# Four buffers for blocks of x, one for loaded q/k, and softmax divisors turned by DMA, in a fused top-k attention and quick-GELU feed-forward kernel

## The chip, the cores and the metric

The kernel runs on one core of one Trainium2 chip. The metric is the device time of one execution in microseconds (us), as the median of several runs. A profiled execution gives a page of tables and a trace. Engines are named as in the profile: PE (TensorE matmul), PEld (its weight load), DVE (VectorE), ACT (ScalarE), POOL (GpSimd), SP (SyncE, which here only issues DMAs, strictly one after the other).

## The reference

Attention over 8 batches, 8 heads, 576 positions and 64 channels that keeps the 32 largest scores of each row, then a feed-forward layer on the joined heads:

```python
scores = (q @ k.T) / sqrt(64)
kth = np.partition(scores, -32, axis=-1)[..., -32:-31]
scores = np.where(scores >= kth, scores, -1e9)
attn = exp(scores - max);  attn = attn / (sum(attn) + 1e-9)
x = (attn @ v)                      # (8, 8, 576, 64) -> (4608, 512)
h = x @ w_in                        # 512 -> 2048
g = h * (1 / (1 + exp(-1.702 * h)))
out = g @ w_out                     # 2048 -> 512
```

Everything is float32.

## The kernel before

**Slots.** The attention is cut into 144 slots, 18 for each batch `b`. A full slot is 128 query rows of two heads (a head pair, `hp` 0 to 3). The last 64 rows of a head pair share a slot with those of another pair. Four full slots with the same 128 rows give one block of x, transposed: a tile `xT` of 128 x 4 x 128 (channels by rows). The 64-row ends of two batches give a block `xT_t`. A block is 128 tokens for the feed-forward layer, and there are 36 of them.

**What a slot does.** PE multiplies q by k into PSUM (`scores`, L281), ACT copies the scores out (`copy_scores`, L293), and DVE finds the 32 largest of each row with MAX8 and MATCH_REPLACE8 on pairwise greater and lesser halves (`topk_of_pairs`, L336, L339; `pair_up`, L322 on DVE and L325, L326 on POOL). ACT then masks (L387) and exponentiates (L390), which also leaves the sums of each row in `sums`. `split` (L461) separates the 16-bit halves, and a DMA writes them to DRAM (`rows`, L463). `turn_by_dma` (L469) reads them back with a DMA transpose into `pt`, which has two buffers. PE multiplies `pt` by v into `o` (`values_at`, L526). These are not yet divided by the sums.

**The divisors.** `invert` (L420, L422 on DVE) makes the reciprocals of the sums of two slots, 128 x 4 numbers with the query row on the partition. The values in `o` lie transposed, with the query row along the free dimension and the channel on the partition, so the divisors have to be turned and repeated over 64 partitions. Before the change POOL repeats them over 64 columns (`wide`, L424), and PE turns that with a transpose per slot (`sum_rows`, L515) into the same PSUM tile as `o`. ACT copies both out to `x` (L902, 128 x 512), and POOL multiplies one by the other into `xT` (`x_of`, L544).

**The feed-forward layer.** `hidden` (L575) multiplies a quarter of `w_in` (16 matmuls of 128 x 128) by the first block in the list `ready`, into PSUM `ph`. ACT takes the tanh (L592) and copies `ph` to `h` (L595), POOL makes the gate from them (`gate`, L604, L605; DVE in the last slots, L607), and PE multiplies it by `w_out` (`project`, L622). A block leaves `ready` after its fourth `hidden`, and its buffer is free then.

**Order.** Each engine's order is written out by hand; nothing is reordered. After an opening and 12 single slots (`slot`), `two_slots(n)` handles slots n and n+1, 68 times from n=12 on. I call one such round a period. On PE a period runs: `hidden`, `project`, the two transposes L515, scores of n+2, values of n-3 and n-2, scores of n+3, `hidden` (into another PSUM pool), `project`. On SP it runs: loads of the first slot, `rows` of n-1, the four DMAs of `prepare_by_dma` if one is due, the transpose `pt` of n-1, the transpose of a prepared q/k pair, loads of the second slot, `rows` of n, `pt` of n, and outputs between them. On POOL the multiplication `x_of` stands between a gate and the next `lesser` (L325, L326). In it `x_of` of a block that begins takes a new `xT` buffer, and with two buffers it waits until PE has done the last `hidden` of the block before the last. At the end `last_slot` works off the remaining blocks.

**Loads of q and k.** `load_both` brings q and k of a head pair (six DMAs) into a tile of the pool `loads`, two buffers. `prepare_by_dma` splits their halves on ACT (L239), writes them to DRAM (L243 to L248) and reads them back transposed (L252). `FETCH` and `READY` (`FETCH_1`, `READY_1` for batch 1) give the slots, counted back from a batch's first slot, in which each pair is loaded and prepared. The pool `raws`, eight buffers, holds `lesser`, `h`, `wide` and `x` in turn.

Of the kernel before, what the change touches and what calls it, by code (L numbers as in the profile page):

```python
# [11 lines left out]
F32 = mybir.dt.float32  # L12
# [4 lines left out]
DRAM = bass.MemoryType.DRAM  # L17

P = 128
# [11 lines left out]
def kernel(  # L31
# [27 lines left out]
    nc = tc.nc  # L59

    B, H, S, D = q.shape
# [3 lines left out]
    NF = S // P  # L65
# [23 lines left out]
    const = ctx.enter_context(tc.tile_pool(name="const", bufs=1))  # L89
    pool = lambda name, bufs, **kw: ctx.enter_context(tc.tile_pool(name=name, bufs=bufs, **kw))  # L90
    raws = pool("raws", 8)
    loads = pool("loads", 2)
    vals = pool("vals", 6)
    qkt = pool("qkt", 6)
    scp = pool("scp", 4)
# [1 line left out]
    lefts = pool("lefts", 2)  # L97
    small = pool("small", 4)
    ptp = pool("ptp", 2)
    xtp = pool("xtp", 2)  # L100
    xtt = pool("xtt", 1)
    thp = pool("thp", 5)
    apart = pool("apart", 4, space=DRAM)
    apart_qk = pool("apart_qk", 2, space=DRAM)
    ps_s = pool("ps_s", 2, space=PSUM)
    ps_t = pool("ps_t", 2, space=PSUM)
    ps_h = pool("ps_h", 1, space=PSUM)
# [2 lines left out]
    ident = const.tile([P, P], F32, name="ident")  # L110
# [6 lines left out]
    raw = {}  # L117
# [42 lines left out]
    loaded = {}  # L160
# [10 lines left out]
    def load(name, b, hp, queue=None):  # L171

        src = q if name == "q" else k
        if (b, hp) not in loaded:
            loaded[b, hp] = loads.tile([P, 2 * NF + 1, 2, D], F32, name="qk_l")
        t = loaded[b, hp]
        if queue is None:
            heads_of = lambda j: of_load(name, t)[:, :, j, :]
        else:
            heads_of = lambda j: heads_apart(name, t)[:, j, :, :]  # L180
        queue = queue or nc.sync
        for j in range(2):
            queue.dma_start(heads_of(j), src[b, 2 * hp + j, 0:FULL, :].rearrange("(p t) d -> p t d", t=NF))

        on = slice(0, TAIL) if name == "q" else slice(TAIL, P)
        queue.dma_start(t[on, 2 * NF, :, :], src[b, 2 * hp : 2 * hp + 2, FULL:S, :].rearrange("h p d -> p h d"))
# [218 lines left out]
    sums = {}  # L405
# [8 lines left out]
    def invert(n):  # L414

        k = (n + 1) // 2
        if k in sums:
            count = 2 if 2 * k < N else 1
            total = sums[k][:, 0:count, :]
            nc.vector.tensor_scalar_add(total, total, 1e-9)  # L420
            inverse = small.tile([P, 2 * count], F32, name="inverse")
            nc.vector.reciprocal(inverse[:], total.rearrange("p s j -> p (s j)"))  # L422
            wide = sums[k] = raws.tile([P, 2, 2, D], F32, name="wide", tag="raw")
            nc.gpsimd.tensor_copy(  # L424
                out=wide[:, 0:count, :, :].rearrange("p s j d -> p (s j) d"),
                in_=inverse[:].unsqueeze(2).to_broadcast([P, 2 * count, D]),
            )

    def turn(n, first, blocks):
        pr = st[n]["pr"]  # L430
# [78 lines left out]
        else:  # L509
            put_off.append(bring)  # L510


    def sum_rows(m, to):

        nc.tensor.transpose(to, sums[(m + 1) // 2][:, (m + 1) % 2, :, :], ident[:])  # L515

    def values_at(m, o):

        b, t, hps = slots[m]
        pt = st[m]["pt"]  # L520
        for p in range(2 if t == NF else 1):
            cols = slice(p * TAIL, (p + 1) * TAIL) if t == NF else slice(0, P)
            main, tail = vv[b, hps[p]]
            for c in range(NF + 1):
                for j in range(2):
                    nc.tensor.matmul(  # L526
                        o[j * D : (j + 1) * D, cols],
                        lhsT=main[:, j, c, :] if c < NF else tail[:, j, :],
                        rhs=pt[:, MAIN[j] + c if c < NF else NF, cols],
                        start=(c == 0),  # L530
                        stop=(c == NF),
                    )
        st[m].clear()
# [32 lines left out]
    def hidden(into=None):  # L566
        if not ready:
            return
        xT, rows = ready[0]
        g = hidden_at["g"]  # L570
        ph = (into or ps_h).tile([P, G, P], F32, name="ph", tag="tp" if into else "ph")
        for i in range(G):
            f = g * G + i
            for c in range(CC):
                nc.tensor.matmul(  # L575
                    ph[:, i, :],
                    lhsT=win[:, c, f * P : (f + 1) * P],
                    rhs=xT[:, c, :],
                    start=(c == 0),
                    stop=(c == CC - 1),  # L580
                )
        to_gate.append((ph, g, rows))
        hidden_at["g"] = (g + 1) % NG
        if g == NG - 1:
            ready.pop(0)

    def tanh(aside):

        if to_gate:
            ph, g, rows = to_gate.pop(0)  # L590
            th = thp.tile([P, G, P], F32, name="th")
            nc.scalar.activation(th[:], ph[:], AF.Tanh, scale=0.851 / RAISE)  # L592
            if aside:
                h = raws.tile([P, G, P], F32, name="h", tag="raw")
                nc.scalar.copy(out=h[:], in_=ph[:])  # L595
                ph = h
            gated.append((th, ph, g, rows))

    def gate(aside):
        if not gated:  # L600
            return
        th, h, g, rows = gated.pop(0)
        if aside:
            nc.gpsimd.tensor_scalar(th[:], th[:], 1.0, 1.0, op0=ALU.add, op1=ALU.mult)  # L604
            nc.gpsimd.tensor_tensor(out=th[:], in0=th[:], in1=h[:], op=ALU.mult)  # L605
        else:
            nc.vector.scalar_tensor_tensor(  # L607
                out=th[:], in0=th[:], scalar=1.0, in1=h[:], op0=ALU.add, op1=ALU.mult
            )
        to_project.append((th, g, rows))  # L610
# [39 lines left out]

    READY = (-12, -10, -4, -2)
    READY_1 = (-6, -4, -3, -2)
    FETCH = (-16, -14, -8, -6)
    FETCH_1 = (-12, -10, -5, -3)
    VALUES = (-2, -1, 1, 2)
    by_slot = dict(enumerate([2, 2, 3, 3, 3, 3, 3, 3, 3, 3, 2, 2]))
    for n in by_slot:
# [170 lines left out]
    def last_slot():  # L828

        tanh(False)  # L830
        gate(False)
        if may_project(0):
            project(range(G))
        hidden()

    def two_slots(n):

        first, second = [later.pop(m, []) for m in (n, n + 1)]
        live = lambda m: 0 <= m < N
        aside = n < N  # L840

        def begin(todo):
            for fn, args in todo:
                if fn is not prepare_by_dma:
                    fn(*args)

        def prepare_some(todo):
            for fn, args in todo:
                if fn is prepare_by_dma:
                    fn(*args)  # L850

        def find(m):
            for i, op in enumerate(topk_of_pairs(m) if live(m) else [lambda: None] * 23):
                op()
                if i == 8 and m % 2 == 0:
                    invert(m - 2)
                if i > 1 and unfinished:
                    finish_one()

        def project_one():  # L860
            if may_project(0):
                project(range(G), True)

        def measure(m):
            if live(m):
                bounds(m)
            gate(aside)

        begin(first)
        measure(n - 1)  # L870
        if live(n - 1):
            exponentials(n - 1)
            split(n - 1)
        bring_all()
        find(n)
        hidden()
        project_one()
        tanh(aside)
        prepare_some(first)
        held = [m for m in (n - 3, n - 2) if live(m) and "rows" in st[m]]  # L880
        o = ps_t.tile([P, 2, 2, P], F32, name="o", tag="tp") if held else None
        for i, m in enumerate(held):
            sum_rows(m, o[:, i, 0, :])
        if live(n + 2):
            scores(n + 2)
            copy_scores(n + 2)
        leave_all()
        for i, m in enumerate(held):
            values_at(m, o[:, i, 1, :])
        if live(n - 1):  # L890
            turn_by_dma(n - 1)
        while turns:
            turns.pop(0)()
        if live(n + 3):
            scores(n + 3)
        begin(second)
        measure(n)
        if live(n):
            exponentials(n)
        if held:  # L900
            x = raws.tile([P, 2, 2, P], F32, name="x", tag="raw")
            nc.scalar.copy(out=x[:, 0 : len(held)], in_=o[:, 0 : len(held)])  # L902
            for i, m in enumerate(held):
                x_of(m, x[:, i, 1, :], x[:, i, 0, :])
        if live(n):
            split(n)
            turn_by_dma(n)
        hidden(ps_t)
        if live(n + 3):
            copy_scores(n + 3)  # L910
        tanh(aside)
        prepare_some(second)
        project_one()
        leave_all()
        find(n + 1)
# [40 lines left out]
```

## Time and profile before

| | us |
|---|---|
| median of 3 runs | 1561.03 (1560.61 to 1563.05) |
| profiled execution | 1561.79 |
| its span, first to last instruction | 1560.0 |
| PE busy | 1461.0 (94%) |
| DVE busy | 1375.2 (88%) |
| ACT busy | 1171.5 (75%) |
| POOL busy | 888.9 (57%) |
| mean granted TensorE clock | 0.972 |

The span is some 1.8 us shorter than the time of the same execution. Busy shares are means over stages. The opening and the 12 single slots take about the first 150 us, the periods run until about 1500 us, and the last slots take the rest. The start of the pair of transposes L515 marks a period on PE, and the distance from one to the next is its length. An idle time in square brackets in a timeline stands in front of the instruction, with what ended it.

### The profile page before, as it was taken

The numbers are of one execution on the slowest core, as the hardware profiler recorded it, in microseconds if no ns is written. First come the engines' busy times: TensorE is split into PE (matmuls) and PEld (weight loads), VectorE is DVE, ScalarE is ACT, GpSimd is POOL, SyncE is SP. The second block draws the span as 40 slices with busy tenths as digits, with TensorE's granted clock in tenths as the row PEclk, the third lists the DMA queues.
The fourth block names the chain that finished last, engine by engine and source line by source line (L and its number), as shares of the span: only waits on it lengthen the run. The fifth ranks groups of instructions, "written<-read, shape, count | busy, mean of one in ns | idle before, by whom it ended". The sixth has DMA issues, their size and how long they took to land. (4 is left out here: it accounts for less than half of the span.)

```text
span 1560.0 us, 31382 instructions
## 1 busy us (share of the span) xinstructions
PE 1461.0 (94%) x10729; PEld 1059.6 (68%) x10729; DVE 1375.2 (88%) x4542; ACT 1171.5 (75%) x1846; POOL 888.9 (57%) x1119
## 2 busy tenths in 40 slices
PE   7789789999999899999998899999998899999997
PEld 5667556777766577777776577777775677777765
DVE  7999989999989799999997799999997889999700
ACT  6998778888768687878786687888876688777710
POOL 3788555666645566666665466666664566666400
PEclk8899899999999999999999999999999999999999
DMA  7451786767755486677767576676765658444500
GB/s 241 134 160 36 194 214 184 194 172 183 189 156 162 126 199 173 173 176 181 187 162 161 128 186 190 163 189 175 179 172 146 161 147 203 131 128 130 145 23 14
DMA packets 533778, 248.35 MB, mean 159 GB/s; under 512 B 465136, under 2 KB 507889, under 8 KB 533617
## 3 DMA queue, kind: packets, MB, share of 16 engines
q1 hardware_dynamic: 533184, 246.05, 60.3%
q8 instruction: 84, 1.38, 0.4%
q14 instruction: 78, 0.63, 0.1%
q10 hardware_dynamic: 432, 0.30, 0.1%
HBM read 45.09 MB, written 105.32 MB: 96 GB/s over the span
## 5 line engine op out<-in xcount | busy, mean ns | idle before, releaser
L622 PE MATMUL po<-wout,th 128*128 128x512 f32 x1152 | 534.2, 608 | 43.9 <-POOL th L605 35.4
L575 PEld LDWEIGHTS ph<-xT,win 128*128 128x128 f32 x4096 | 473.9, 192 | 69.6 <-issue 53.2
L575 PE MATMUL ph<-xT,win 128*128 128x128 f32 x4096 | 489.3, 277 | 12.3 <-POOL xT L544 12.3
L622 PEld LDWEIGHTS po<-wout,th 128*128 128x128 f32 x1152 | 213.5, 195 | 264.5 <-issue 216.4
L336 DVE MAX8 top<-left 128x8 f32<-128x288 f32 x792 | 325.3, 445 | 0.0
L461 ACT COPY sc<-pr 128x2304 uint16<-128x2304 uint16 x133 | 281.5, 2117 | 2.2
L293 ACT ACTIVATE sc<-s_ps 128x576 f32<-128x576 f32 x288 | 172.2, 654 | 140.6 <-PE s_ps L281 130.3
L544 POOL TENSOR_TENSOR xT<-x 128x128 f32<-128x128 f32 x117 | 51.7, 458 | 392.6 <-DVE top L343 215.1
L390 ACT ACTIVATE pr<-sc,low 128x576 f32<-128x576 f32 x288 | 220.6, 774 | 47.7 <-POOL low L367 47.7
L336 DVE MAX8 top<-lesser 128x8 f32<-128x288 f32 x528 | 214.1, 446 | 37.1 <-POOL lesser L326 37.1
L339 DVE MATCH_REPLACE8 left<-top,left 128x288 f32<-128x288 f32 x528 | 229.6, 442 | 0.0
L387 ACT ACTIVATE sc<-sc,cut 128x576 f32<-128x576 f32 x288 | 208.7, 783 | 2.7 <-POOL cut L378 2.1
L326 POOL TENSOR_TENSOR lesser<-lesser,greater 128x576 int32<-128x576 int32 x132 | 186.0, 1409 | 22.7 <-DVE greater L322 13.2
L325 POOL TENSOR_TENSOR lesser<-sc 128x576 int32<-128x576 int32 x132 | 187.6, 1421 | 0.0
L281 PE MATMUL s_ps<-qk_t 64*128 64x288 f32 (+1 forms) x1280 | 185.2, 436 | 1.0 <-ACT sc L293 0.8
L605 POOL TENSOR_TENSOR th<-th,h 128x512 f32<-128x512 f32 x127 | 161.9, 1275 | 10.6
L526 PE MATMUL o<-pt,v_l 128*64 128x128 f32 (+1 forms) x2384 | 147.5, 268 | 11.0 <-DMA pt<-rows 11.0
L526 PEld LDWEIGHTS o<-pt,v_l 128*64 128x64 f32 x2384 | 122.7, 139 | 38.1 <-issue 22.9
L592 ACT ACTIVATE th<-ph 128x512 f32<-128x512 f32 x144 | 86.6, 602 | 81.0 <-PE ph L575 80.9
L322 DVE TENSOR_TENSOR greater<-sc 128x576 f32<-128x576 f32 x132 | 104.6, 792 | 44.7 <-ACT sc L293 35.4
L281 PEld LDWEIGHTS s_ps<-qk_t 64*128 64x128 f32 (+1 forms) x1280 | 100.8, 180 | 42.6 <-issue 22.1
L339 DVE MATCH_REPLACE8 left<-top,greater 128x288 f32<-128x288 f32 x264 | 114.8, 442 | 0.0
(86 smaller groups left out, 1606.2 us busy)
## 6 DMA issues: line engine op xcount, KB each, us to landing
rows<-sc SPq DMA_DIRECT2D x133, 576.0 KB, 3.1
qk_rows<-halves SPq DMA_DIRECT2D x56, 256.0 KB, 2.8
qk_l<-in_q_dram SPq DMA_DIRECT2D x64, 128.0 KB, 3.0
raw<-in_moe_w_in_dram SPq DMA_DIRECT2D x16, 512.0 KB, 5.2
v_l<-in_v_dram SPq DMA_DIRECT2D x32, 256.0 KB, 3.2
raw<-in_moe_w_out_dram SPq DMA_DIRECT2D x16, 512.0 KB, 3.6
out_dram<-ob SPq DMA_DIRECT2D x32, 256.0 KB, 2.9
qk_l<-in_k_dram SPq DMA_DIRECT2D x62, 128.0 KB, 2.9
```

The lines of the kernel that those rows point to most:

```text
L281: nc.tensor.matmul(ps[i][rows, c, 0:HALF], lhsT=qT[b, hps[p]][on, cols], rhs=kT[b, hps[p]][on, FIRST[i] + c * HALF : FIRST[i] + (c + 1) * ...
L293: nc.scalar.mul(out=to, in_=ps[i][:, :, 0:HALF], mul=SCALE)
L325: nc.gpsimd.tensor_tensor(out=whole, in0=a.bitcast(I32), in1=b.bitcast(I32), op=ALU.add)
L326: nc.gpsimd.tensor_tensor(out=whole, in0=whole, in1=greater[n][:].bitcast(I32), op=ALU.subtract)
L336: nc.vector.max(top[:, i, 8 * r : 8 * r + 8], src[:, i, :])
L339: nc.vector.match_replace(to[:, i, :], top[:, i, 8 * r : 8 * r + 8], src[:, i, :], LOWEST)
L387: nc.scalar.activation(sc[:, i, :], sc[:, i, :], AF.Prelu, bias=cut[:, i : i + 1], alpha=HUGE)
L390: nc.scalar.activation(pr[:, i * S : (i + 1) * S], sc[:, i, :], AF.Exp, bias=low[:, i : i + 1], accum_out=den[:, i : i + 1],)
L461: nc.scalar.copy(out=halves, in_=pr[:].bitcast(U16).rearrange("p (k h) -> p h k", h=2))
L526: nc.tensor.matmul(o[j * D : (j + 1) * D, cols], lhsT=main[:, j, c, :] if c < NF else tail[:, j, :], rhs=pt[:, MAIN[j] + c if c < NF else ...
L575: nc.tensor.matmul(ph[:, i, :], lhsT=win[:, c, f * P : (f + 1) * P], rhs=xT[:, c, :], start=(c == 0), stop=(c == CC - 1),)
L622: nc.tensor.matmul(po[:], lhsT=gT[:, i, :], rhs=wout[:, f, :], start=(f == 0), stop=(f == FC - 1))
```

## The change

`xtp`, the pool of `xT`, gets four buffers in place of two, and `loads` one in place of two. In batch 0 the loads of odd head pairs go into the pool of `pt`, whose buffers have the same size. `FETCH` and `FETCH_1` move so that each load follows the preparation of the pair before it.

The divisors are no longer repeated by POOL and transposed by PE. `invert` issues a DMA on SP that writes the 128 x 4 reciprocals to DRAM (`lines`) with the query row along the line. The new function `spread` issues two DMAs on SP that read these lines back, each repeated over 64 partitions, into a tile `by` of the pool `raws`. The PSUM tile `o` and its copy `x` halve to 128 x 256.

In `last_slot` the next `hidden` comes ahead of the gate and `project` of the one before, and the two take turns in two PSUM pools.

```diff
-    loads = pool("loads", 2)
+    loads = pool("loads", 1)
-    xtp = pool("xtp", 2)
+    xtp = pool("xtp", 4)
+    apart_by = pool("apart_by", 2, space=DRAM)
...
-            loaded[b, hp] = loads.tile([P, 2 * NF + 1, 2, D], F32, name="qk_l")
+            home, tag = (ptp, "pt") if b == 0 and hp % 2 else (loads, "qk_l")
+            loaded[b, hp] = home.tile([P, 2 * NF + 1, 2, D], F32, name="qk_l", tag=tag)
...
-            wide = sums[k] = raws.tile([P, 2, 2, D], F32, name="wide", tag="raw")
-            nc.gpsimd.tensor_copy(
-                out=wide[:, 0:count, :, :].rearrange("p s j d -> p (s j) d"),
-                in_=inverse[:].unsqueeze(2).to_broadcast([P, 2 * count, D]),
+            lines = apart_by.tile([2, 2, P], F32, name="lines")
+            nc.sync.dma_start(lines[0:count].rearrange("s j q -> q (s j)"), inverse[:])
+            sums[k] = lines, count
+
+    def spread(n):
+
+        lines, count = sums.pop((n + 1) // 2)
+        by = raws.tile([P, 2, P], F32, name="by", tag="raw")
+        for j in range(2):
+            nc.sync.dma_start(
+                by[j * D : (j + 1) * D, 0:count, :],
+                lines[0:count, j, :].unsqueeze(0).to_broadcast([D, count, P]),
             )
+        return by
...
-    def sum_rows(m, to):
-
-        nc.tensor.transpose(to, sums[(m + 1) // 2][:, (m + 1) % 2, :, :], ident[:])
...
-    FETCH = (-16, -14, -8, -6)
-    FETCH_1 = (-12, -10, -5, -3)
+    FETCH = (-16, -11, -8, -3)
+    FETCH_1 = (-12, -5, -3, -2)
...
     def last_slot():
 
         tanh(False)
+        hidden(ps_t if hidden_at["g"] % 2 else None)
         gate(False)
         if may_project(0):
             project(range(G))
-        hidden()
...
-        o = ps_t.tile([P, 2, 2, P], F32, name="o", tag="tp") if held else None
-        for i, m in enumerate(held):
-            sum_rows(m, o[:, i, 0, :])
+        by = spread(held[0]) if held else None
+        o = ps_t.tile([P, 2, P], F32, name="o", tag="tp") if held else None
...
-            values_at(m, o[:, i, 1, :])
+            values_at(m, o[:, i, :])
...
-            x = raws.tile([P, 2, 2, P], F32, name="x", tag="raw")
+            x = raws.tile([P, 2, P], F32, name="x", tag="raw")
...
-                x_of(m, x[:, i, 1, :], x[:, i, 0, :])
+                x_of(m, x[:, i, :], by[:, (m + 1) % 2, :])
```

## The prediction

> **What bounds the kernel now.** I read the page first: PE is busy for 94% of the span. Then the waits, for what stops PE, and the timeline, for where. The lines below come in that order: page, waits, three windows (length, then busy time of PE, PEld, DVE, ACT, POOL, granted clock, DMA share, GB/s), and pieces of the timeline.
>
> ```profile
> PE 1461.0 (94%) x10729; PEld 1059.6 (68%) x10729; DVE 1375.2 (88%) x4542; ACT 1171.5 (75%) x1846; POOL 888.9 (57%) x1119
> ...
> qk_l<-in_q_dram SPq DMA_DIRECT2D x64, 128.0 KB, 3.0
> ```
>
> ```profile
> POOL xT L544 <- PE ph L575: 55.4, 6, 9.2
> PE po L622 <- POOL th L605: 35.4, 7, 5.8
> ```
>
> ```profile
> 448.30:475.40 27.10, 21.28 (x140) 14.80 (x139) 20.40 (x72) 18.29 (x25) 12.61 (x16) 0.87 0.56 150
> 1120.95:1140.05 19.10, 19.10 (x140) 13.92 (x139) 18.77 (x67) 15.09 (x24) 10.82 (x14) 1.00 0.78 192
> 1407.60:1427.70 20.10, 19.30 (x155) 13.65 (x154) 19.67 (x69) 15.21 (x24) 10.79 (x14) 1.00 0.41 109
> ```
>
> ```profile
> 829.04 0.45 POOL L544 TENSOR_TENSOR xT<-x 128x128 f32<-128x128 f32 x1 [9.21 <-PE ph L575]
> ...
> 834.78 5.78 PE L622 MATMUL po<-wout,th 128*128 128x512 f32 x8 [5.83 <-POOL th L605]
> ```
>
> ```profile
> 1061.34 0.35 SPq L463 DMA_DIRECT2D rows<-sc  x1
> 1062.54 0.38 PE L515 MATMUL o<-ident,wide 128*128 128x128 f32 x2
> 1062.85 1.24 PE L281 MATMUL s_ps<-qk_t 64*128 64x288 f32 x8
> 1065.38 2.83 SPq L469 DMA_TRANSPOSE pt<-rows  x1
> 1068.05 0.57 ACT L902 COPY x<-o 128x512 f32<-128x512 f32 x1
> 1068.70 0.88 POOL L544 TENSOR_TENSOR xT<-x 128x128 f32<-128x128 f32 x2 [4.82 <-DVE top L343]
> 1077.22 1.41 POOL L326 TENSOR_TENSOR lesser<-lesser,greater 128x576 int32<-128x576 int32 x1
> 1077.85 0.82 DVE L343 TENSOR_TENSOR top<-top 128x32 f32<-128x32 f32 x1
> ```
>
> ```profile
> 186.10 1.26 SPq L183 DMA_DIRECT2D qk_l<-in_q_dram  x2
> 187.75 2.13 ACT L239 COPY halves<-qk_l 128x2304 uint16<-128x2304 uint16 x1
> 1517.69 3.70 PE L622 MATMUL po<-wout,th 128*128 128x512 f32 x8 [1.41 <-DVE th L607]
> ```
>
> The starts of the L515 pairs give 66 period lengths, of three kinds. Most take 19.11, and PE has no gap in them (second window): PE is the bound, and DVE, at 18.77, is right behind. Sixteen take about 20.1: `hidden` follows in the same period on the block that `x_of` has just finished, and PE waits some 0.7 for it. Six take 27.07, 27.83, 27.27, 27.93, 27.32 and 27.95: there POOL waits for an `xT` buffer (9.21 above), everything behind it on POOL is late, and PE ends 5.8 idle and goes on at a lower clock (0.87 in the first window). The first few periods, to about 254, are not full on PE and go by SP, ACT and DVE.
>
> **The change part by part.**
>
> **1. Four `xT` buffers.** In the order written out, the six long periods are those in which a block begins one period before the block two places earlier has had its last `hidden`. With four buffers the block that must be gone is two older, gone four or more periods before. The wait then has no cause. The six lengths sum to 165.37, against 6 x 19.11 = 114.66: **-50.7**. Where does the stall go? Into PE, whose periods on both sides already last 19.11 without a gap. This takes the loss of clock with it.
>
> **2. No L515, no `wide`.** From the first L515 to the scores behind it is 1062.54 to 1062.85, 0.31. It is on PE's path in the 62 periods or so after 254: at most 19.2. DVE could cap this at 18.77. But its merge L343 takes 0.82 there beside POOL's L326, and 0.19 at 1068.52, where POOL rests, so it can lose 0.63; `wide` takes up to 0.96 on POOL just ahead and L326 moves up by as much as that goes. If the divisors are late by part of a microsecond the merge stays long, and only 19.11 - 18.95 = 0.16 is had, 18.95 being two DVE searches of 9.21 and 9.98 (starts 800.33, 810.31, 819.52) less their 0.24 of waits. Between 9.9 and 19.2 I take **-15**, nearer the upper end because in most periods `by` is in time by item 4. The smaller `x` copy is on ACT, which has over 3 us idle in a period: nothing.
>
> **3. The last slots.** Five times PE waits 1.41 for tanh and gate (1517.69 and every 8.68 after). With the next `hidden` in front, 3.6 of matmuls cover this; behind the last one lies the `project` before it, 3.4. Without that cover it would be 1.41 each again. **-7.05**.
>
> **4. Divisors through DRAM.** Per period SP gains three DMAs: `lines` behind `rows` of n-1, `by` twice behind the q/k DMAs, and the `by` issue waits until `lines` has landed. Queued behind it on SP are an output, `pt` of n-1 and the q/k transpose. `pt` of n-1 moves from 1065.38 to about 1066.3 and is wanted by PE one period later: covered by some 12 us. `pt` of n, which is nearest to its use, has about 2.6 us left in the periods with loads of item 5.
> The one that waits for `by` is POOL's `x_of`, at 1068.70. No row shows `lines` (512 runs of 4 bytes). The nearest is a q load, also 512 runs: 3.0 from issue to landing, 0.62 to issue. Below I bound it by the shortest landing of the page, 2.1, above by the q/k transpose, 5.0. `by` has 64 KB in 512-byte runs, nearest the small loads at 2.6 to 2.7. From `rows` at 1061.34: `lines` issued at 1061.75; behind `rows` on the same queue, so I add 0.4 to 3.1, the landing of `rows`: 3.5; second `by` issued 0.5 later; 2.7 to land: 1068.45. The margin is 0.25. Ends: 2.1 and 2.1 give 1066.4, 2.3 early; 5.0 and 5.0 give 1072.2, 3.5 late. Lateness L counts fully in the sixteen just-in-time periods; in the others POOL has cover until DVE wants `lesser`: L326 ends at 1072.44 and is read at 1075.43, so some 2.9. In the six of the sixteen with a q/k preparation ahead of `by` (qk_rows issued 1081.52 to 1083.74), `by` is issued at 1083.8 to 1084.8 and lands at about 1087.5, against `x_of` at 1087.80. I take 0.3 for each of sixteen: **+5**, ends 0 and, with 3.5, 56 plus 50 x 0.6 = 30, so 86.
>
> The Trainium skill, "DMA: Bandwidth & Descriptors", speaks against this: "Rules for kernel authors" says that a strided last dimension becomes one descriptor per element, and "Bandwidth" gives about 10.5 ns per packet, beside some 2.0 us fixed. My estimate from the page is 512 x 10.5 ns = 5.4, so 7.4 for `lines`, and `by` would be late by 3.65: 16 x 3.65 + 50 x 0.75, some 96 us, in place of 5. The trace argues otherwise: 465136 packets under 512 bytes go almost wholly to 161 transposes, over 2700 each, landed in 4.8 to 5.0. Whether 4-byte writes behave so, no row here shows.
>
> **5. One buffer for loads.** In batches 2 to 7 a load sits in the period before its preparation. Loads at -11 and -3 move to the second half and go ahead of `rows` of n: six DMAs of 0.6 delay that by some 3 us, `pt` of n to a landing near 1101.7 where PE wants it near 1104.3. Covered: 0, and 12 x 2 = 24 if the cover is gone. In batch 1 pairs 2 and 3 are loaded in the very slot of their preparation. Before, ACT's L239 ran at 187.75; now the load can only be issued at about 187.6 and lands near 194: 6 us in which ACT stands, with the score copies behind it and DVE waiting for those. The next pair adds some 3. DVE is near its limit there, so this counts, less what SP catches up meanwhile (PE also waits 6.0 for a `pt` at 225). Ends 0 and 14: **+7**. In batch 0 one short SP wait goes: nothing.
>
> Sum: 1560.0 - 50.7 - 15 - 7.05 + 5 + 7 = 1499.2. The profiled execution took 1.8 more than its span and the median 0.8 less than that: **1500**.
>
> **The rivals.**
>
> *Divisors late.* `lines` and `by` both at 5.0: 1500 + 86 - 5 = 1581 at the very end; at 3.8 for both, lateness is 1.4: 16 x 1.4 = 22 in place of 5, 1517. I put it at **1540**, lateness 2.7. For it: 0.25 of margin. Against: small DMAs here land in 2.1 to 3.1.
>
> *Loads late.* Item 5 at its upper ends, 14 and 24: **1531**. For it: 2.6 us of cover on an SP queue in which a transpose alone takes 2.4 to 2.8. Against: only 3 waits of PE for `pt` in the whole trace (11 us).
>
> *Slower.* The 4-byte writes of `lines` in DRAM don't overlap, and SP, which stands still until they land, and POOL both stop each period. Without item 4 the sum is 1495, so it takes 66 to undo the gain: with L the landing of `lines`, 16(L-3.75) + 50(L-6.65) = 66 gives L = 6.95. At 8 the time is 1495 + 68 + 67 = **1630**. For it: no row has such writes. Against: 8 is 1.6 times the longest landing of a transpose.
>
> *The stall isn't gone.* If something else held `xT` in the six periods, the gain is items 2 and 3 alone less 12: **1551**. Against it: POOL's wait there names PE's L575, the release of that buffer.
>
> **How the numbers follow.** Chances: forecast 0.60 (its own range 1486 to 1513), divisors late 0.16, loads late 0.12, stall not gone 0.03, slower 0.09. Range: from 1485 (item 2 at 19.2, items 4 and 5 near 0 and 2) up to 1545, which takes in the loads and most of the late divisors. A measurement can tell about 0.2%, 3 us, from no change. Below 1558: all but the last case and a little: 0.89; within: 0.02; slower: 0.09.
>
> **What would show it.** No wait of POOL's `xT` for PE's L575, no period over 21 us after 254, and a granted clock of 1.00 there; full periods of 18.8 to 19.0; last slots without a gap on PE. Item 4 is wrong if POOL's `xT` waits for DMA `by` for more than 1 us in most periods, or `lines` lands after more than 4 us. Item 5 is wrong if PE waits for `pt` in the periods with -11 or -3, or if ACT's L239 near 190 doesn't wait. The whole is wrong if full periods get longer than 19.11.

## The result and the profile after

| | before | after |
|---|---|---|
| median of 4 runs, us | 1560.82 (1560.53 to 1563.05) | 2051.39 (2049.78 to 2054.23) |
| ratio | | 1.3141 [1.3118, 1.3164] |
| span of the profiled execution | 1560.0 | 2049.0 |
| mean granted TensorE clock | 0.972 | 0.873 |

The changed kernel is 31% slower; 1500 was predicted. The page of the kernel after: busy times by engine, the chain that ended last by line, and the costliest group of POOL.

```profile
PE 1573.2 (77%) x10596; PEld 1114.9 (54%) x10596; DVE 1400.4 (68%) x4542; ACT 1164.1 (57%) x1846; POOL 840.2 (41%) x1052
...
DMA lines<-inverse 8%; PE po L629 4%; PE ph L582 4%; DMA by<-lines 4%; SPq L434 1%; DVE top L338 1%; POOL lesser L328 1%; POOL lesser L327 1%; DVE top L345 1%; SPq L480 1%; ACT sc L472 1%; POOL xT L551 1%; ACT pr L392 0%; DVE lesser L341 0%; DMA rows<-sc 0%
...
L551 POOL TENSOR_TENSOR xT<-x,by 128x128 f32<-128x128 f32 x117 | 55.2, 490 | 858.2 <-DMA by<-lines 846.1
```

No engine is the bound any more: PE falls from 94% to 77%, and the chain leads through the two transfers of the divisors. The multiply L551 itself takes 490 ns, little more than before (458); it stands idle for 858 us ahead of it. The waits of the kernel after (engine, line, what it waited for: us in total, times, longest):

```profile
POOL xT L551 <- DMA by<-lines: 846.1, 58, 20.3
DVE top L338 <- POOL lesser L328: 342.4, 63, 11.4
ACT pr L392 <- POOL low L369: 280.6, 48, 12.7
...
PE po L629 <- POOL th L612: 251.1, 45, 10.3
```

One cause and three consequences: POOL waits for `by`, and DVE's search (`lesser`), ACT's exponentials (`low`) and PE's second layer (`th`) wait for what POOL does behind it. No wait of POOL's `xT` for PE's first layer is left. The waits of SP's own queue:

```profile
SPq L434 <- DMA lines<-inverse: 475.9, 54, 11.4
SPq L480 <- DMA rows<-sc: 187.8, 66, 4.5
```

SP stands 8.8 us on average in 54 periods before it may issue `by`. One period in the timeline (start, duration, engine, line, operation; in brackets the idle time in front):

```profile
1105.98 0.38 SPq L426 DMA_DIRECT2D lines<-inverse  x1
...
1108.97 1.03 SPq L250 DMA_DIRECT2D qk_rows<-halves  x1
...
1109.62 0.37 ACT L908 COPY x<-o 128x256 f32<-128x256 f32 x1 [1.35 <-PE o L533]
...
1118.23 1.27 SPq L434 DMA_DIRECT2D by<-lines  x2
...
1119.60 2.62 SPq L480 DMA_TRANSPOSE pt<-rows  x1
1121.87 0.87 POOL L551 TENSOR_TENSOR xT<-x,by 128x128 f32<-128x128 f32 x2 [18.84 <-DMA by<-lines]
...
1128.03 5.49 PE L629 MATMUL po<-wout,th 128*128 128x512 f32 x8 [5.70 <-POOL th L612]
```

`lines` is issued at 1105.98 and `by` can follow only at 1118.23, 12.25 later. SP has nothing to do from 1110.0 on, and the transpose `pt` waits behind `by`. POOL has had its `x` since 1110.0 and starts at 1121.87. The distance from the issue of `lines` to that of `by` is 9.0 to 12.6 in all 67 periods, 10.9 in the middle. The prediction had 3.5 for the landing of `lines`.

The single packets in the trace show where this time goes. In the period above the 512 writes of `lines` are over 2.6 us after its issue, some 9 ns each. What stands behind them hardly moves: packets of 512 bytes, which take 0.03 us in the middle of the run, take up to 4.4 us each there (`qk_rows`, L250 above). From 300 to 1300 us, 1219 packets of 512 bytes take over 0.5 us; in e1 of the next section none does. So most of the 10.9 us comes after the packets of `lines` are over.

The windows from 300 to 1300 us (length, then busy time of PE, PEld, DVE, ACT, POOL, granted clock, DMA share, GB/s) show the loss of clock that comes with it; after, and then e1 of the next section:

```profile
300.00:1300.00 1000.00, 766.14 (x5131) 533.89 (x5129) 693.78 (x2318) 567.05 (x867) 406.54 (x517) 0.87 0.62 130
```

```profile
300.00:1300.00 1000.00, 990.77 (x7472) 719.19 (x7472) 971.32 (x3322) 811.79 (x1235) 618.66 (x790) 1.00 0.69 179
```

### The profile page after: what moved, and what is told of

Its sections match the earlier page's. It is cut to its first block, busy times and chain, and to the rows that moved or that the text cites. A ratio compares the mean times of both kernels' runs of the same rounds, so it can differ in the third digit from the quotient of the medians.

```text
span 2049.0 us, 31423 instructions
## 1 busy us (share of the span) xinstructions
PE 1573.2 (77%) x10596; PEld 1114.9 (54%) x10596; DVE 1400.4 (68%) x4542; ACT 1164.1 (57%) x1846; POOL 840.2 (41%) x1052
## 5 line engine op out<-in xcount | busy, mean ns | idle before, releaser
L629 PE MATMUL po<-wout,th 128*128 128x512 f32 x1152 | 607.6, 677 | 252.5 <-POOL th L612 251.1
L582 PE MATMUL ph<-xT,win 128*128 128x128 f32 x4096 | 528.0, 290 | 146.8 <-POOL xT L551 144.0
L582 PEld LDWEIGHTS ph<-xT,win 128*128 128x128 f32 x4096 | 511.4, 204 | 205.9 <-POOL xT L551 147.3
L629 PEld LDWEIGHTS po<-wout,th 128*128 128x128 f32 x1152 | 240.6, 220 | 521.6 <-POOL th L612 259.6
L551 POOL TENSOR_TENSOR xT<-x,by 128x128 f32<-128x128 f32 x117 | 55.2, 490 | 858.2 <-DMA by<-lines 846.1
L611 POOL TENSOR_SCALAR th<-th 128x512 f32<-128x512 f32 x127 | 78.7, 620 | 97.0 <-ACT th L599 97.0
```

What stands on the lines that cost most here:

```text
L582: nc.tensor.matmul(ph[:, i, :], lhsT=win[:, c, f * P : (f + 1) * P], rhs=xT[:, c, :], start=(c == 0), stop=(c == CC - 1),)
L629: nc.tensor.matmul(po[:], lhsT=gT[:, i, :], rhs=wout[:, f, :], start=(f == 0), stop=(f == FC - 1))
```

## The experiments

Edits are against the changed kernel unless another is named. Those marked "single run" were timed once; the others are medians of four runs.

### Which part of the change costs

**e1**: divisors by POOL and PE as before (`wide`, `sum_rows`), the rest of the change kept.

```diff
-            lines = apart_by.tile([2, 2, P], F32, name="lines")
-            nc.sync.dma_start(lines[0:count].rearrange("s j q -> q (s j)"), inverse[:])
+            wide = sums[k] = raws.tile([P, 2, 2, D], F32, name="wide", tag="raw")
+            nc.gpsimd.tensor_copy(...)
...
-        by = spread(held[0]) if held else None
+            sum_rows(m, o[:, i, 0, :])
```

> The change without its divisor part: POOL repeats and PE turns the divisors as before; four xT buffers, one load buffer, new fetch slots and the new last slots stay. Theory W (the 4-byte writes of the lines to DRAM take about 10 us to be acknowledged, and that alone makes the kernel slow): the other terms of the prediction hold, 1560 - 50.7 - 7.05 + 7 = 1509 us, full periods 19.11. Rival L (the single load buffer and the later fetches hold SP and ACT up in all batches): well over 1560, with waits of ACT for loads of q/k and of PE for pt in every batch.

Measured: 1513.07 (1511.05 to 1519.12), ratio 0.9700 [0.9674, 0.9726], span 1509.3. The sum of items 1, 3 and 5 gave 1560.0 - 50.7 - 7.05 + 7 = 1509.25. These 1509.3 are the fastest of the four runs; by the medians e1 gains 49.2 us over the kernel before in the same round (1562.28), where the sum has 50.75. All of the loss, 538 us from e1 to the change, comes with the new way of the divisors, items 4 and 2. The waits of e1 on the places of items 1 and 5:

```profile
ACT halves L240 <- DMA qk_l<-in_k_dram: 13.6, 3, 6.6
...
PE ph L576 <- POOL xT L545: 11.6, 16, 0.8
```

The wait for a load that item 5 foretold is there (6.6 at the longest): the reciprocal of n = 44 starts at 465.7, and at 458.4 before, 7.3 later. PE's wait for the block just finished stays, 16 times some 0.7. No period after 254 is over 21 us; the six had 27 to 28.

**e12**: the kernel before with the new order of the last slots alone.

```diff
         tanh(False)
+        hidden(ps_t if hidden_at["g"] % 2 else None)
         gate(False)
...
-        hidden()
```

> The kernel before with the new order of the last slots alone. The prediction's term: five waits of 1.41 go, 1561 - 7.05 = 1554 us. Rival: PE waits elsewhere for the gate or for the second PSUM pool: 1557 to 1561.

Measured: 1554.24 (1553.67 to 1555.92) beside 1562.07, ratio 0.9952 [0.9935, 0.9968]: 7.8 less, as item 3 has it (7.05).

### Why `lines` lands so late

**e2** (single run): `lines` as runs of 16 bytes, 128 of them, in the order in which `inverse` lies; `by` then gets divisors of other rows.

```diff
-            nc.sync.dma_start(lines[0:count].rearrange("s j q -> q (s j)"), inverse[:])
+            nc.sync.dma_start(lines[0:count].rearrange("s j q -> (s j q)").rearrange("(q w) -> q w", w=2 * count), inverse[:])
```

> As the changed kernel, but the reciprocals are written to DRAM in their own order, 128 runs of 16 bytes in place of 512 of 4 bytes (so the divisors stand at wrong places and the output is not the reference's); all other DMAs, their sizes and waits are the same. Theory W: the time from the issue of the lines to the issue of the first by falls from a median of 10.9 us; to about 3 if the number of separate writes sets it (a quarter of 512, so some 10.9/4 or the 2.1 to 3.1 of other small landings), and the kernel takes 1500 to 1530 us. Rival Q (the lines are late because they stand behind the rows on SP's queue, whatever their shape): it stays near 10 us, and the kernel near 2050.

Measured: 1615.48. The DMA issues of e2 (KB each, median us from issue to landing):

```profile
by<-lines SPq DMA_DIRECT2D x132, 64.0 KB, 2.8
...
lines<-inverse SPq DMA_DIRECT2D x66, 2.0 KB, 3.2
```

The landing is now what the prediction assumed (3.5 and 2.7), and 436 of the 538 us are gone. But 102 over e1 are left, where the expectation had at most 17: a second cause.

**e3** (single run): `lines` issued by ACT instead of SP.

```diff
-            nc.sync.dma_start(lines[0:count].rearrange("s j q -> q (s j)"), inverse[:])
+            nc.scalar.dma_start(lines[0:count].rearrange("s j q -> q (s j)"), inverse[:])
```

> As the changed kernel, but ACT issues the DMA of the lines in place of SP, so that it goes through another queue than the rows written just before it. Theory W: the landing stays at 9 to 12 us and the kernel within some 5% of 2050. Rival Q: the landing falls to about 3 us and the kernel to about 1500.

Measured: 1954.87. Where SP stood at `by`, 10.7 us lay between the issue of `lines` and that of `by`. So the place behind `rows` on SP's queue isn't the cause. And SP's queue is not left alone: ten transposes `pt` are issued by SP within 4 us of ACT's `lines`, and all ten take 6.3 to 8.8 us to be issued, 2.6 in the middle of all. One of them:

```profile
952.85 0.37 ACTq L426 DMA_DIRECT2D lines<-inverse  x1
954.55 8.80 SPq L480 DMA_TRANSPOSE pt<-rows  x1
```

**e6, e11, e7** (a single run each) keep 4-byte runs. e6 puts each run into 64 bytes of its own, e11 four runs into 64 bytes (the change has 16). e7 writes the divisors of one slot only, 256 runs as densely as the change has them. In all three `by` gets other numbers than the divisors in part.

```diff
+    lines_of = [apart_by.tile([2, 2, P, 16], F32, name=f"lines{i}") for i in range(2)]
-            nc.sync.dma_start(lines[0:count].rearrange("s j q -> q (s j)"), inverse[:])
+            nc.sync.dma_start(lines[0:count, :, :, 0].rearrange("s j q -> q (s j)"), inverse[:])
```

```diff
+            nc.sync.dma_start(lines[0].rearrange("j q -> q j"), inverse[:, 0:2])
```

The first diff is e6's (e11 has 4 in place of 16), the second e7's.

> As the changed kernel, but each 4-byte reciprocal is written into 64 bytes of its own (by reads the first 512 bytes of each line, so the divisors are not the reference's). Theory W1 (each separate short write has its price in DRAM): the time from the lines' issue to by's stays at 9 to 12 us, the kernel near 2050. Rival W2 (neighbouring 4-byte writes to the same 64 bytes hold each other up): it falls to 3 to 5 us, the kernel towards 1615.

> As e6, but each 4-byte reciprocal has 16 bytes of its own, so four share 64 bytes in place of one (e6) or sixteen (the changed kernel). Theory W2 (writes to the same 64 bytes wait for each other): the price per further write is (10.9 - 3.3) / 15 = 0.5 us, so lines to by where SP stands there takes 3.3 + 3 x 0.5 = 4.8 us. If it were a threshold (any sharing costs the whole): 10.9.

> As the changed kernel, but only the first slot's divisors are written, 256 runs of 4 bytes (and by takes them for both slots, so half of the divisors are wrong). Theory W: the landing goes with the number of short writes, from 10.9 to about 2 + 8.9/2 = 6.5 us, and the kernel to about 1800. If the 4-byte form has a fixed price, it stays near 10.9.

One period of SP's timeline in each, e6 and then e7:

```profile
1039.24 0.38 SPq L427 DMA_DIRECT2D lines<-inverse  x1
1042.87 1.93 SPq L435 DMA_DIRECT2D by<-lines  x2
```

```profile
1022.41 0.38 SPq L426 DMA_DIRECT2D lines<-inverse  x1
1032.66 1.29 SPq L434 DMA_DIRECT2D by<-lines  x2
```

| | 4-byte runs | in each 64 bytes | `lines` to `by`, middle, us | time |
|---|---|---|---|---|
| change | 512 | 16 | 10.9 | 2051.39 |
| e7 | 256 | 16 | 10.25 | 2101.41 |
| e11 | 512 | 4 | 4.1 | 1646.75 |
| e6 | 512 | 1 | 3.3 | 1718.33 |

(e6 and e11: of those periods in which SP stood.) Half as many runs cost the same, and as many runs farther apart cost a third. So it is not their number but how close they lie: 4-byte writes to DRAM that fall into the same stretch hold each other up. (For e11, 4.8 was expected if the price goes by the number that share 64 bytes, and 10.9 if any sharing cost the whole.) In e6 the 512 writes are over as early as in the change, 2.4 us after the issue in the middle of all periods, and only 43 packets of 512 bytes take over 0.5 us. How long such a stretch is was not tried; 64 bytes is only the unit of these runs. e6 is slower than e11 although its `lines` lands sooner; its `by` lands after 4.6 instead of 2.9, its transposes after 5.6 instead of 4.8. The two ran on different chips, and why wasn't tried. e7's time was missed by 300 us, because fewer runs were expected to land sooner.

### What is left when `lines` lands in 3 us

**e4**: VectorE turns the reciprocals (blocks of 32 x 32), so that `lines` has runs of 128 bytes. `by` then takes four fetches a period. **e5**: the same, all five transfers issued by ACT. **e8** (single run): e2 with `by` issued by ACT.

```diff
+            turned = small.tile([P, 32], F32, name="turned")
+            nc.vector.transpose(turned[:], inverse[:])
+            lines = apart_by.tile([4, 32, 32], F32, name="lines")
+            nc.sync.dma_start(lines[:].rearrange("b c q -> (b c) q"), turned[:])
```

> As the changed kernel, but DVE turns the reciprocals in blocks of 32 x 32 before the DMA, so that the lines go to DRAM as 128 runs of 128 bytes; four smaller DMAs (128-byte runs) bring them back in place of two. It computes the reference. Theory W: the lines land in about 3 us; full periods 18.8 to 19.1, total 1495 to 1530. Rival Q: landing near 10 us, total near 2050. If 128-byte runs suffer as 4-byte ones do, something between.

> As e4_turned_by_dve, but ACT issues the lines and the four by; SP has then just the work that it had before the change. Theory S (SP issues one DMA after the other and stands at each wait; lines, the wait for their landing and by push its work past a period, so that SP sets the period): the period falls back to 18.8 to 19.2 and the kernel to 1495 to 1515 us, though lines and by go through DRAM as in e4. Rival C (the chain inverse, lines, by, multiplication is too long in itself): POOL still waits for by in most periods and the kernel stays above 1600.

> As e2_runs_of_16_bytes, but ACT issues the two by, and so waits for the lines in SP's place; SP keeps the one short issue of the lines. Theory S: from 1615 to 1500 to 1530 us. Rival C: no change, near 1615.

Measured: e4 1703.22, ratio 1.0902 [1.0881, 1.0924]; e5 1588.23, ratio 1.0158 [1.0123, 1.0193]; e8 1674.23. In e4 `lines` lands in 2.6, and the kernel is still slower than before. Taking the transfers off SP (e5) gives 115 us back, but now ACT spends 3.0 us a period on issuing the five and stands at `by` for 68 us in all. Its score copies come late (DVE waits 85 us for them, 29 in e1), and what POOL's `xT` waits for is now ACT's copy `x` (in e1 127.8, and 184.5 for DVE's merge):

```profile
POOL xT L556 <- ACT x L913: 325.9, 55, 14.5
```

In e8 ACT's score copies come late too (DVE waits 179 us for them, 65 in e2). A wait that is moved from one serial queue to another stays a wait; both expectations were missed.

**e9, e10**: `invert` half a period earlier, ahead of `pt` of n, with 4-byte runs (e9) and with e4's (e10).

```diff
-                if i == 8 and m % 2 == 0:
-                    invert(m - 2)
...
+        invert(n)
```

> As the changed kernel, with the same 4-byte writes, but the reciprocals of slots n-1 and n are made and written right behind the rows of n, at the start of DVE's next search, some 7 us earlier and ahead of a transpose pt that waits on SP for those rows anyway. Theory S (SP stands at by until the lines have landed, and that sets the period; the 10.9 us themselves do no harm where SP needn't stand): the lines land before SP comes to by, or nearly; full periods 18.8 to 19.0, total 1490 to 1515 us. Rival (a landing of 10.9 us blocks the queue or memory for what follows wherever it stands): above 1700, with pt and the rows landing late.

> Both together: reciprocals turned by DVE in blocks of 32 x 32, written as 128-byte runs right behind the rows of n, four by per period on SP. Theory S: SP never stands at by; but two more issues of by per period (about 0.6 each) on SP and 128-byte reads: 1490 to 1530 us.

Measured: e9 1940.48, ratio 1.2419 [1.2395, 1.2442]; e10 1724.69, ratio 1.1051 [1.1026, 1.1077]. SP no longer stood at `by` (e9 6 us in all, e10 none). Two things stood in the way. The edit was badly placed: DVE, in order, waited for exponentials that weren't done (`sums` for `pr`: 475 us in e9, 276 in e10). And e9 shows something new in SP's timeline:

```profile
1005.30 0.39 SPq L426 DMA_DIRECT2D lines<-inverse  x1
1008.16 10.68 SPq L480 DMA_TRANSPOSE pt<-rows  x1
```

e10 has the same order with runs of 128 bytes:

```profile
1027.45 0.38 SPq L430 DMA_DIRECT2D lines<-turned  x1
1030.01 2.32 SPq L485 DMA_TRANSPOSE pt<-rows  x1
```

The 66 transposes that come right behind `lines` take 8.7 us to be issued in the middle and up to 10.68 in e9; in e10 they take 2.5, and none over 3.04. The 4-byte writes stop not only those who wait for them, but also what comes next.

**e13, e14, e15**: `invert` at the end of DVE's search of the odd slot, where the sums are ready, with e4's runs of 128 bytes (e13), the change's 4-byte runs (e14), and e2's runs of 16 bytes (e15, single run).

```diff
-                if i == 8 and m % 2 == 0:
-                    invert(m - 2)
+                if i == 22 and m % 2:
+                    invert(m - 1)
```

> The kernel of e4 (inverses turned by VectorE, runs of 128 bytes, four fetches of `by` on SP), with the inverse taken at the end of VectorE's search of the odd slot, where the sums are ready, so that `lines` goes out ahead of the next period's rows. Theory S (what is left beyond the landing is SP standing at `by`, with everything behind it): SP stands near nothing at `by`, VectorE does not wait for the sums, 1495 to 1530 us. Rival P (the chain from the sums to the first layer, by four transfers in a row, is too long for where the first layer reads it, wherever it begins): 1600 or more.

> The change itself with its 4-byte writes; only the inverse is moved to the end of VectorE's search of the odd slot, as in e13. Theory S: `lines` has some 8 us more before `by` is issued, SP stands 2 to 3 us where it stood 8: 1500 to 1560. Rival B (4-byte writes hold up whatever is issued behind them on the queue by 10 us, wherever they stand): the fetch or the transpose behind `lines` takes some 10 us to be issued, 1650 or more.

> e2 (runs of 16 bytes, two fetches of `by`; the divisors land at wrong places) with the inverse at the end of VectorE's search of the odd slot, as in e13. Theory S: near 1500, since neither the landing (3.2) nor a standing SP is left. Rival P: as e2, 1600 or more.

Measured: e13 1657.25, ratio 1.0617 [1.0591, 1.0642]; e14 1916.94, ratio 1.2287 [1.2246, 1.2329]; e15 1571.9. The earlier place gives 46 us with e4's runs, 134 with the change's, 44 with e2's. With 4-byte runs the blocking stays, now on `rows`, which follows `lines`; the waits of e14 (54.5 us in all in the change, 2.6 in e1):

```profile
ACT sc L295 <- DMA rows<-sc: 165.3, 37, 9.0
```

That SP's standing is all that is left is false: e15 stands at `by` for 30 us in all and is still 61 slower than e1 in span. Its timeline shows why POOL still waits for `by` (224 us):

```profile
1012.19 0.18 DVE L424 RECIPROCAL inverse<-sums 128x4 f32<-128x4 f32 x1
...
1013.22 0.36 SPq L474 DMA_DIRECT2D rows<-sc  x1
...
1016.11 2.76 SPq L480 DMA_TRANSPOSE pt<-rows  x1
...
1019.29 0.34 SPq L426 DMA_DIRECT2D lines<-inverse  x1
```

The reciprocals are ready at 1012.37, and SP comes to `lines` at 1019.29, after `rows`, its landing, and `pt`. In the middle of all periods 10.7 us pass, and with q/k loads ahead up to 16.9. SP is a serial queue without slack there.

**e16, e17, e18** price this. e16 is e1 with `lines` (16-byte runs) and two fetches that wait for it, which nobody reads. e17 is the same with fetches from q, which wait for nothing. e18 keeps the reader: e13 with `lines` issued by ACT right behind the search, and a layout that needs two fetches.

```diff
+            lines = apart_by.tile([2, 2, P], F32, name="lines")
+            nc.sync.dma_start(lines[0:count]..., inverse[:])
...
+            nc.sync.dma_start(
+                idle_by[j * D : (j + 1) * D, 0:count, :],
+                lines[0:count, j, 0:80].unsqueeze(0).to_broadcast([D, count, 80]),
+            )
```

```diff
-            lines = apart_by.tile([4, 32, 32], F32, name="lines")
-            nc.sync.dma_start(lines[:].rearrange("b c q -> (b c) q"), turned[:])
+            lines = apart_by.tile([32, 4, 32], F32, name="lines")
+            nc.scalar.dma_start(lines[:].rearrange("c b q -> b c q"), turned[:])
```

The first diff is e16's, the second e18's.

> e1 (divisors by GpSimd and TensorE, as before; 1513) with the three transfers added on SP for nobody to read: `lines` in runs of 16 bytes and two fetches that wait for it, of runs of 320 bytes. GpSimd waits for none of them. Theory S (SP standing at `by`, and what is queued behind it): 1550 to 1600 us. Rival L (SP's issuing time alone, some 2 us a period): as e17. Rival P (only the chain that a reader waits for): 1509 to 1520.

> e16 with the two unread fetches taken from q in DRAM, so that they wait for nothing. Rival L: 1540 or more, as SP issues some 2 us more a period. Theory S: near e1, 1510 to 1525, since SP does not stand. Rival P: 1509 to 1520.

> e13 with `lines` issued by ScalarE right behind VectorE's search, where ScalarE waits for the search in any case, and with a layout of `lines` that needs two fetches of `by` instead of four (each of 512 bytes). SP issues two small transfers a period instead of five and hardly stands. Theories S and L: 1510 to 1550, near e1. Rival P: 1570 or more, as e15.

Measured: e16 1550.88, ratio 0.9930 [0.9906, 0.9954]; e17 1544.90, ratio 0.9887 [0.9862, 0.9911]; e18 1547.58, ratio 0.9907 [0.9889, 0.9925]. The waits of e17, and then of e16's SP queue:

```profile
PE o L543 <- DMA pt<-rows: 30.2, 15, 4.2
```

```profile
SPq L441 <- DMA lines<-inverse: 118.1, 52, 3.9
```

Transfers that nobody waits for cost 31.8 us (1544.90 - 1513.07), as rival L has it: PE's wait for `pt` rises from 6.3 in e1 to 30.2, and DVE's for the score copies from 28.8 to 55.3. The likeliest cause is SP's issuing time, some 1.9 us a period, since a transpose still takes 2.5 to be issued and 4.7 to land (4.6 in e1); what the moved bytes themselves cost was not separated. That SP also stands for 118 us adds only 6.0. The readers add the rest. e18, with the divisors in place, has e13's reader 110 us cheaper, by both of its differences at once; what POOL still waits is in its waits:

```profile
POOL xT L555 <- DMA by<-lines: 133.9, 22, 8.0
```

It is 0.9% faster than before, but 34.5 slower than e1. Of the kernels measured with the whole computation, e1 is the fastest: all of the change except item 4 and, with it, item 2.

## Why the prediction was wrong

The steps from e1 to the changed kernel, each from the medians above:

| step | us | time |
|---|---|---|
| e1: items 1, 3, 5 | | 1513.1 |
| three more DMAs a period on SP (e17) | +31.8 | 1544.9 |
| two of them wait for `lines`, 3.3 (e16) | +6.0 | 1550.9 |
| POOL reads them, L515 and `wide` gone (e2) | +64.6 | 1615.5 |
| runs of 4 bytes instead of 16 (the change) | +435.9 | 2051.4 |

The fetches of e16 and e17 have runs of 320 bytes, those of e2 512, and e2 is a single run, so the middle steps aren't exact. A period of e1 with loads ahead of `rows` on SP, for item 4's third term below:

```profile
934.99 0.58 SPq L198 DMA_DIRECT2D v_l<-in_v_dram  x1
935.62 1.11 SPq L206 DMA_DIRECT2D v_e<-in_v_dram  x2
936.77 1.27 SPq L184 DMA_DIRECT2D qk_l<-in_q_dram  x2
...
940.81 0.54 SPq L468 DMA_DIRECT2D rows<-sc  x1
...
944.21 0.87 POOL L545 TENSOR_TENSOR xT<-x 128x128 f32<-128x128 f32 x2 [6.62 <-DVE top L344]
```

- **Item 1** (-50.7), **item 3** (-7.05) and **item 5** (+7) came out as worked: together 49.2 of 50.75 us in e1. The six long periods were the buffers of `xT`, and the rival "stall isn't gone" fell. So did "loads late": PE waits 6.3 us for `pt` in e1, 11.0 before.
- **Item 2** (-15) can't be read from the result, and no run has it alone. It lies inside the +64.6.
- **Item 4 (+5) is the step that failed**, in its first term above all: "from `rows` at 1061.34 ... `lines` ... 3.5", with ends 2.1 and 5.0. It was priced by the nearest row with the same number of runs, a q load. That row reads DRAM, in runs of 256 bytes; `lines` writes DRAM, in runs of 4. Measured: 10.9. The transposes, which the prediction called as a witness for many small packets, read DRAM as well.
- The skill's estimate that stood beside it, 7.4 for `lines` (the Trainium skill, "DMA: Bandwidth & Descriptors", "Bandwidth"; the fixed 2.0 in it stands under "Anatomy of one DMA"), was nearer, but not by its mechanism: with so much per packet, e7's 256 runs should land after some 4.7, and e6's 512 after 7.4; they measured 10.25 and 3.3. The same page says in "Anatomy of one DMA", of DMAs issued by GpSimd, that a DMA counts as done only when the target memory has confirmed its last byte, and "This can cause a surprisingly long delay especially when the write target is HBM". That agrees with the packets, which are over some 8 us before the landing, though it gives no price. The target alone doesn't explain it: `rows` is written to DRAM too and lands in 3.1 before.
- **Item 4's second term**, SP's own time, was set at nothing, "covered by some 12 us". The three transfers on SP cost 31.8 before anybody reads them (e17). The 12 us are those of `pt` of n-1 in one period; that `pt` of n has but 2.6 us left in periods with loads was written down and not priced. In e17, 14 of PE's 15 waits for `pt` come behind loads of q, k or v on SP.
- **Item 4's third term**, the cover of 2.9 on POOL in the periods that aren't just in time: with `lines` landing in 3.2 it should have cost next to nothing, and the readers cost 64.6 (e2). `lines` did go out right behind `rows` (0.5 us after it in the middle, in e2). But the sum took the time from `rows` to `x_of` from one period, 7.36 us, of which it needs 7.1. Where loads of q, k and v stand ahead of `rows` on SP, `rows` itself is late. In the period of e1 above, `x_of` follows 3.4 us after `rows`. In 27 of 59 periods of e1 the copy `x` is ready less than 7 us after `rows`, in 14 less than 5. `by` would be late in them even with the landing as predicted.
- **The rival "slower"** had the mechanism, writes that don't overlap, SP standing, POOL stopped, and its break-even at 6.95. It was given 0.09, because 8 seemed far from the longest landing of a transpose. At the measured 10.9 its formula gives 1495 + 16 x 7.15 + 50 x 4.25 = 1822. The other 229 it had no term for; e17 and e9 show two that are missing: three more transfers on SP, and the transfers that stop behind 4-byte writes.
- Of what would show item 4 wrong, both came: `lines` lands after more than 4, and POOL waits for `by` in 58 periods. Full periods got longer too, which was to show the whole wrong: 27.6 us in the middle, against 19.11.

What stays open: item 2's worth, how e17's 31.8 divide between SP's issuing time and the bytes moved, how long the stretch of DRAM is in which writes collide, and how the last 34.5 of e18 divide between SP's issuing and the reader.

## What to carry to other kernels

An operation that no row of the trace shows is not priced by a row that shares its count. Direction (read or write of DRAM), run length and spacing have to match too, and if none does, the upper end must reach to where the sign turns. A DMA with a wait in the middle of a serial queue costs three times over: its issue, the standing of all behind it, and the lateness of its own chain (here some 32, 6 and 65 us). So before a small on-chip operation is replaced by a trip through DRAM, count the issues and waits of that queue in its fullest stretch, not in a single period.

## What the runs showed of the hardware

- 4-byte writes to DRAM, 16 to 64 bytes, took 10.9 us to land (512 of them) and 10.25 (256); 512 took 4.1 with four to 64 bytes and 3.3 with one. 128 runs of 16 bytes landed in 3.2. In the dense layout and in the widest the 512 packets themselves are over 2.4 us after the issue, in the middle of all periods.
- Dense 4-byte writes hold up the next DMA: transposes right behind them took 8.7 us to issue in the middle and up to 10.68 (e9), at the same place behind 128-byte runs at most 3.04 (e10). It isn't a matter of one queue: behind `lines` on ACT's queue, SP's transposes took 6.3 to 8.8 (e3).
- With the engines starved, the granted clock fell with PE's load: 0.87 from 300 to 1300 us after, 1.00 in e1.
